# Slot logits of a fused attention and soft mixture of experts: small products from a transposed f16 copy of the attention output, in place of 32 extra columns of the value products

## The chip, the cores and the metric

The kernel runs on one core of a Trainium2 chip. The core has a matrix engine (PE, whose weight loads the profile lists apart as PEld), three engines for elementwise work and reductions (DVE, ACT, POOL) and a queue engine (SP) that issues most DMA transfers. Each engine works through its instructions in a fixed order and waits for others by semaphores. PE writes its results to PSUM, which DVE and ACT read; POOL works on SBUF only. The metric is the device time of one execution in microseconds (us); lower is better.

## The reference

Four batches of 12288 queries attend to 768 pooled keys, whose values are the keys themselves. The attention output x (49152 rows of 128) then goes through a soft mixture of experts with 32 slots. The slot logits `x @ phi` are what the change is about.

```python
kv_pool = kv.reshape(B, H // r, r, W // r, r, C).mean(axis=(2, 4))
k = v = kv_pool.reshape(B, -1, C) @ w_sr
s = scale * (q @ k.transpose(0, 2, 1))
a = np.exp(s - s.max(-1, keepdims=True))
x = (a / (a.sum(-1, keepdims=True) + 1e-09)) @ v
...
logits = x @ phi                                # 32 slots
d = softmax(logits over all rows)               # dispatch
slot_out = relu((d.T @ x) @ w1[e]) @ w2[e]      # per expert
out = softmax(logits over the slots) @ slot_out # combine
```

## The kernel before

The queries are cut into 96 blocks of 512 (`NB`), four blocks to a group; the last group is cut into one of three blocks and one of a single block, so that there are 25 groups. For each block:

- PE multiplies keys and queries into three PSUM tiles `s0`, `s1`, `s2` of two banks each (`qk`, L476 to L478: each operand is split into a high and a low part, so three products for each 128 keys, 18 of 512 columns in a block). There is one buffer of each, so the next block's products into `s0` wait until DVE has subtracted the maximum from this block's.
- DVE takes the row maximum: three reductions of 128x1024 (`rowmax1`, L483), a short reduction and a product (L493, L495), then a small PE product with a selector (`rowmax_pe`, L503), a reduction of its result (L508), and a transpose that spreads the maximum (`rowmax4`, L513). Four subtractions (`sub`, L521) then free the PSUM tiles. From L495 to L508 DVE waits for PE unless other DVE work is put there.
- ACT computes the exponential twice for each half of the block (`exp_hi` to f16, L528, and `exp_t` to f32, L532), POOL the low part of it as their difference (`plo`, L537).
- PE multiplies the probabilities with the values (`av_hi`, L554 and L555, and `av_lo`, L562): for each of four slices of 128 queries 12 products with the high part and 6 with the low part, 72 in a block. The right-hand side has 161 columns (160 in L555): one column of ones for the row sum, 128 of values, and 32 of `v @ phi`, which were made once per batch from a widened weight (`w_sb`, 160 columns: L368, and L799 at the start). The 32 last columns of the result are the slot logits before the division by the row sum.
- ACT copies the result, two slices at a time, from PSUM to the group's tile `xl` (`av_evac`, L572, 128x322).

The PSUM space outside `s0` to `s2` is two banks (`m0`, `m1`), which the value products, the row maximum's small product and all else share.

After the last block of a group, `group_ops` runs some twenty short steps: the logits are scaled into `LL` (`g1l`, POOL, L626), their column maximum is taken (L631, L633, L661 to L668, with a small PE product L654), weights are formed (L673 to L690) and 16 (for a full group) times two PE passes sum them with x (`g7m`, L707, 32 matmul records), which DVE adds to `acc` (L713). A reciprocal of the row sums (L609) is the DVE step near the start of it, and the row maximum for the combine (`k_max`, L718) a later one. Keys and values of the next batch are made while a batch runs (`kv_ops`; L347 to L440). After the last block come the experts and the combine.

The order on PE, DVE, ACT and POOL is made when the program is built: every step is an `op(...)` with a cost, a latency, a priority and its dependences and buffers; `Plan.emit` goes through them with these numbers and writes each engine's instructions in the order it finds. On the chip the order stands, and times are what they are. SP's queue is in order too: loads of q (1 MB for a group, two buffers) and of kv, then weights and results.

Of the kernel before, what the change touches and what calls it, by code (L numbers as in the profile page):

```python
# [172 lines left out]
def attention_then_soft_moe(ctx: ExitStack, tc: tile.TileContext, qT, kv0, kvT, w_sr, w_srT, phi, w1, w2, outT):  # L173
# [20 lines left out]
    FAST = len(GB) - 2  # L194
    VW = C + 1 + NS
# [40 lines left out]
    nc.vector.memset(epk, EPS * PK)  # L236
# [39 lines left out]
        "pooled": 1, "v32": 1, "r6": 2, "rq": 2, "m1": 2, "mb": 1, **{f"s{u}": 1 for u in range(NU)},  # L276
# [84 lines left out]
    def kv_v_mm(b, h):  # L361
        if h == 0:
            VU[b] = bp.tile([P, NT, C + NS], F32, tag="v32", name=f"v32_{b}", bufs=1)
        pv = mt([P, 512], f"pv_{b}_{h}")
        pv3 = PK_[b, h, "v"] = pv[:, : 3 * (C + NS)].rearrange("p (t c) -> p t c", t=3)
        for t in range(3):
            kt = 3 * h + t
            nc.tensor.matmul(pv3[:, t, :], pooled[b][:, kt * P : (kt + 1) * P], w_sb, start=True, stop=True)  # L368

    def kv_v_out(b, h):  # L370
        nc.scalar.activation(VU[b][:, 3 * h : 3 * h + 3, :], PK_.pop((b, h, "v")), AF.Copy, scale=1.0 / R2)

    def kv_m(b, k, h):
# [11 lines left out]
        if h and k:  # L385
            nc.vector.tensor_reduce(out=am2, in_=am, axis=X, op=ALU.max)
# [5 lines left out]
    def kv_s_mm(b):  # L392
        pa = PK_[b] = mt([P, 512], f"pa_{b}")
        nc.tensor.matmul(
            pa[:, : 2 * P], ones, AM.pop(b)[1].rearrange("p k n -> p (k n)"), start=True, stop=True
        )

    def kv_s_g(b):
        pa = PK_.pop(b)
        pg = pa[:, 2 * P : 2 * P + 2]  # L400
        nc.vector.tensor_reduce(out=pg, in_=pa[:, : 2 * P].rearrange("p (k n) -> p k n", k=2), axis=X, op=ALU.max)
# [138 lines left out]
    def av_tile(i, k):  # L540
        if k % 2 == 0 and i == NB - 1:
            PX[i, k // 2] = ps.tile([P, 2, BQ], F32, tag=f"s{k // 2}", name=f"px_{i}_{k}")[:, :, :VW]
        elif k % 2 == 0:
            px = mt([P, 512], f"px_{i}_{k}")
            PX[i, k // 2] = px[:, : 2 * VW].rearrange("p (n c) -> p n c", n=2)
        return PX[i, k // 2][:, k % 2, :]

    def av_hi(i, k):
        _, vhi, vlo = VU[i // BPB]
        px = av_tile(i, k)  # L550
        ks = slice(k * P, (k + 1) * P)
        for t in range(NT):
            p = PP[i, t // TH][0][:, t % TH, ks]
            nc.tensor.matmul(px, p, vhi[:, t, :], start=(t == 0), stop=False)  # L554
            nc.tensor.matmul(px[:, 1:], p, vlo[:, t, :], start=False, stop=False)  # L555

    def av_lo(i, k):
# [3 lines left out]
        for t in range(NT):  # L561
            nc.tensor.matmul(px, PP[i, t // TH][1][:, t % TH, ks], vhi[:, t, :], start=False, stop=(t == NT - 1))  # L562

    def av_evac(i, k):
# [3 lines left out]
        o = (i - GB[g][0]) * TB + 2 * k  # L568
        if i == NB - 2 and k == 0:
            nc.vector.tensor_copy(XL[g][:, o : o + 2, :], PX.pop((i, k)))  # L570
        else:
            nc.scalar.activation(XL[g][:, o : o + 2, :], PX.pop((i, k)), AF.Copy)  # L572
# [23 lines left out]
    def g0(g):  # L596
# [4 lines left out]
        if g > FAST:  # L601
            nc.vector.tensor_scalar_add(xc, xc, EPS * PK)
# [219 lines left out]
    def kv_ops(b, base, step, dep0, dep1):  # L822
# [10 lines left out]
        m = {0: [], 1: []}  # L833
        for h in range(2):
# [5 lines left out]
            for k in range(2):  # L840
                m[k].append(op("DVE", (0.53 if k == 0 else 0.2) + 0.2 * h * k, 0.08, p + step * (1 + 0.4 * k), [at_["vo", h]] + m[k] + m[0][:1], lambda h=h, k=k: kv_m(b, k, h), use=[("v32", b)]))
        d = [op("ACT", 0.4, 0.1, base + step * 5, m[0] + m[1], lambda k=k: kv_d(b, k)) for k in range(2)]
        s = op("PE", 0.6, 0.4, base + step * 5.5, d, lambda: kv_s_mm(b), acq=[("m", ("pa", b))])
        s = op("DVE", 1.1, 0.08, base + step * 5.5, [s], lambda: kv_s_g(b), use=[("m", ("pa", b))])
        prev = [s] + dep1
        for k in range(2):
# [3 lines left out]
            prev = [a]  # L850

    kv_ops(0, -60, 1.5, [[ops["pool", 0, R2 - 2], ops["wo"]], [ops["pool", 1, R2 - 2], ops["wo"]]], [])

    def group_ops(g):
# [5 lines left out]
        base = HEAD + (e + 2.6) * PER  # L860
# [5 lines left out]
        deps = [ops["x", e, 1]]  # L866
        if g >= 2:
# [21 lines left out]
        go("1l", big, bg(), [o["1u"]], g1l)  # L889
# [363 lines left out]
```

## Time and profile before

| | us |
|---|---|
| runs (two) | 1116.43 and 1115.16, median 1115.8 |
| profiled execution, first to last instruction | 1112.9 |
| PE busy / PEld busy | 1044.9 / 893.6 |
| DVE busy | 984.2 |
| ACT busy | 829.4 |
| POOL busy | 870.5 |

The profiled execution is one run of the program; its own time is known as the span alone, 2.9 us below the median of the runs. Busy shares are averages over a start that loads and pools the first keys (about 30 us), 96 blocks, and an end (from about 1005 us on) with the experts and the combine. Names of tiles are the program's, without buffer numbers; `m` is one of the two shared banks. A record of a matmul lasts longer than its place in the pipeline: what it costs is the distance from one start to the next.

### The profile page before, as it was taken

Reading aid. Unit: us, or ns where it says so; the run is one execution under the profiler, and the core shown is the slowest. Engines: PE = TensorE matmul, PEld = TensorE weight load, DVE = VectorE, ACT = ScalarE, POOL = GpSimd, SP = SyncE. Lnnn points to the kernel's source line nnn. Section 1 sums busy time; section 2 is a strip of 40 time slices with the busy share of each in tenths; the row PEclk is TensorE's granted clock in tenths of the full one; section 3 lists DMA queues with packets and bytes.
Section 4 is the critical chain, followed back from the end, with each engine's and each line's share of the span. In section 5 each row is a group of like instructions: output and inputs, shape, how many; then the busy total and the mean of one; then the engine's idle time right before and its main releaser. Section 6 shows DMA issues by size and latency. Waiting matters only on the chain.

```text
span 1112.9 us, 24732 instructions
## 1 busy us (share of the span) xinstructions
PE 1044.9 (94%) x10198; PEld 893.6 (80%) x10198; DVE 984.2 (88%) x1493; ACT 829.4 (75%) x1029; POOL 870.5 (78%) x503
## 2 busy tenths in 40 slices
PE   3699999999999999999999999999999999997885
PEld 2588888888888888888888888888888888886343
DVE  7889889899889989899888988989989988997894
ACT  1677778778777878778777788688778777875563
POOL 0679898798899889789899989789889889873440
PEclk9899999999999999999999999999999999999975
DMA  9218301111136310120145310120110110113498
GB/s 351 108 31 177 70 16 39 39 58 39 39 60 150 82 35 6 39 87 10 39 102 108 82 39 1 39 95 2 39 39 1 39 39 2 39 39 114 145 406 357
DMA packets 17407, 89.15 MB, mean 80 GB/s; under 512 B 1680, under 2 KB 3984, under 8 KB 11152
## 3 DMA queue, kind: packets, MB, share of 16 engines
q1 hardware_dynamic: 13408, 69.47, 17.0%
q0 software_dynamic: 3312, 17.70, 8.4%
q8 instruction: 81, 1.33, 0.5%
q10 hardware_dynamic: 576, 0.41, 0.1%
q14 instruction: 30, 0.25, 0.1%
HBM read 58.87 MB, written 25.17 MB: 76 GB/s over the span
## 4 chain that ended last, share of the span: by engine, by line
PE 61%; ACT 18%; DVE 15%; issue 3%; POOL 2%; DMA 1%; SPq 0%; DVEq 0%; ACTq 0%
PE m L562 10%; PE m L554 10%; PE m L555 9%; ACT phi L528 8%; PE s L476 8%; PE s L478 7%; PE s L477 7%; ACT t L532 7%; DVE t L521 4%; PE m L503 3%; DVE r L483 3%; PE m L707 2%; PE po L1138 2%; DVE o L1147 2%; DVE mb L513 1%
## 5 line engine op out<-in xcount | busy, mean ns | idle before, releaser
L537 POOL TENSOR_TENSOR plo<-t,phi 128x1536 f16<-128x1536 f32 x190 | 598.8, 3156 | 128.1 <-ACT t L532 127.3
L528 ACT ACTIVATE phi<-t,lnk 128x1536 f16<-128x1536 f32 x192 | 301.5, 1570 | 118.9 <-DVE t L521 118.7
L483 DVE TRANSPOSE_TENSOR_REDUCE r<-s 128x32 f32<-128x1024 f32 x288 | 348.6, 1233 | 29.3 <-PE s L478 25.7
L554 PE MATMUL m<-vhi,phi 128*128 128x161 f16 x2280 | 354.7, 234 | 2.8 <-DVE acc L713 1.4
L555 PE MATMUL m<-vlo,phi 128*128 128x160 f16 x2280 | 353.8, 233 | 0.0
L521 DVE TENSOR_TENSOR t<-s,mb 128x1024 f32<-128x1024 f32 (+1 forms) x384 | 342.8, 949 | 9.3
L532 ACT ACTIVATE t<-t,lnk 128x1536 f32<-128x1536 f32 x192 | 301.5, 1570 | 3.6
L476 PE MATMUL s<-qhi,khi 128*128 128x512 f32 x576 | 239.9, 417 | 6.1 <-DVE t L521 5.8
L554 PEld LDWEIGHTS <-phi 128*128 128x128 f16 x2304 | 224.3, 98 | 24.3 <-issue 24.3
L555 PEld LDWEIGHTS <-phi 128*128 128x128 f16 x2304 | 225.1, 98 | 5.4 <-issue 3.5
L562 PE MATMUL m<-vhi,plo 128*128 128x161 f16 x2280 | 226.5, 234 | 0.4 <-POOL plo L537 0.4
L478 PE MATMUL s<-qhi,klo 128*128 128x512 f32 x576 | 226.6, 393 | 0.0
L477 PE MATMUL s<-qlo,khi 128*128 128x512 f32 x576 | 226.1, 392 | 0.0
L562 PEld LDWEIGHTS <-plo 128*128 128x128 f16 x2304 | 178.2, 100 | 1.2 <-POOL plo L537 0.6
L466 POOL TENSOR_TENSOR qlo<-q,qhi 128x512 fp32r<-128x512 f32 x96 | 128.6, 1340 | 26.8 <-ACT qhi L462 26.8
L572 ACT ACTIVATE xl<-m 128x322 f32<-128x322 f32 x189 | 81.4, 430 | 84.5 <-PE m L562 83.8
L476 PEld LDWEIGHTS s<-qhi,khi 128*128 128x128 f32 x576 | 109.2, 190 | 32.6 <-issue 7.5
L478 PEld LDWEIGHTS s<-qhi,klo 128*128 128x128 f32 x576 | 108.8, 189 | 24.7 <-DVE klo L356 0.5
L477 PEld LDWEIGHTS s<-qlo,khi 128*128 128x128 f32 x576 | 109.5, 190 | 18.7 <-issue 0.7
L513 DVE STREAM_TRANSPOSE mb<-m 128x512 f32<-128x512 f32 x96 | 68.3, 711 | 3.3
L462 ACT ACTIVATE qhi<-q 128x512 fp32r<-128x512 f32 x96 | 59.1, 616 | 1.5 <-issue 0.8
L508 DVE TENSOR_REDUCE m<-m 128x16 f32<-128x64 f32 x96 | 21.5, 224 | 40.7 <-PE m L503 40.7
(145 smaller groups left out, 860.1 us busy)
## 6 DMA issues: line engine op xcount, KB each, us to landing
q<-qT SPq DMA_DIRECT2D x23, 1024.0 KB, 4.8
outT<-o SPq DMA_DIRECT2D x21, 1024.0 KB, 5.4
kva<-kvT POOLq DMA_DIRECT2D x9, 1536.0 KB, 11.2
kva<-kvT SPq DMA_DIRECT2D x3, 1536.0 KB, 10.5
kv<-kv SPq DMA_DIRECT2D x8, 512.0 KB, 5.6
w<-w SPq DMA_DIRECT2D x2, 1536.0 KB, 6.4
w<-w SPq DMA_DIRECT2D x4, 768.0 KB, 4.4
outT<-o SPq DMA_DIRECT2D x6, 512.0 KB, 4.7
```

Of the source, the lines that this page charges most:

```text
L466: nc.gpsimd.tensor_tensor(out=lo, in0=q_src(i), in1=hi.bitcast(F32), op=ALU.subtract)
L476: nc.tensor.matmul(s, khi[:, ks], hi, start=True, stop=False)
L477: nc.tensor.matmul(s, khi[:, ks], lo, start=False, stop=False)
L478: nc.tensor.matmul(s, klo[:, ks], hi, start=False, stop=True)
L483: nc.vector.tensor_reduce(out=MX[i][:, 2 * u : 2 * u + 2, :].rearrange("p t b -> p (t b)"), in_=S[i, u].rearrange("p t (b j) -> p (t b) j" ...
L521: nc.vector.tensor_tensor(out=TT_[i, h][:, o : o + n, :], in0=S[i, t // 2][:, u : u + n, :], in1=MX[i].unsqueeze(1).broadcast_to([P, n, BQ ...
L528: nc.scalar.activation(hi, TT_[i, h], AF.Exp, bias=lnk, scale=SCALE)
L532: nc.scalar.activation(t, t, AF.Exp, bias=lnk, scale=SCALE)
L537: eng.tensor_tensor(out=lo, in0=TT_.pop((i, h)), in1=PP[i, h], op=ALU.subtract)
L554: nc.tensor.matmul(px, p, vhi[:, t, :], start=(t == 0), stop=False)
L555: nc.tensor.matmul(px[:, 1:], p, vlo[:, t, :], start=False, stop=False)
L562: nc.tensor.matmul(px, PP[i, t // TH][1][:, t % TH, ks], vhi[:, t, :], start=False, stop=(t == NT - 1))
```

## The change

For blocks 0 to 91 (`i < OLD`) the value products have 129 and 128 columns. The logits of such a block come in five new steps: ACT scales the attention output by 1/2048 and rounds it to f16 (`x_hi`, twice a block, 128x256), DVE forms the f16 rest (`x_lo`, twice, 128x256, from PSUM), SP issues a DMA that transposes both parts (`x_t`, 128x1024 f16, 256 KB, SBUF to SBUF), PE multiplies four 128x128 pieces with the high and low parts of phi (`l_mm`, 12 products of 32 columns into a shared bank), and ACT copies the 128x128 result into `xl` (`l_out`). `av_evac` is two slices of 129 columns for these blocks. Blocks 92 to 95 keep the 32 extra columns; the last batch therefore keeps its 160-column weight, and the other three make 128 columns and one maximum instead of two.

Around it: `av_hi` is given to the order in pieces of two 128-key tiles (`AVS`), which it can place apart; phi is scaled and split once at the start (`phi_m` to `phi_l`); the group steps start later (3.1 instead of 2.6 block lengths) and `g1l` waits for all `l_out` of the group; and the descriptor memory of POOL's DMAs is set to 8192.

```diff
+    OLD = GB[FAST][0]
...
+        w = VWB(b) - 1
...
-            nc.tensor.matmul(pv3[:, t, :], pooled[b][:, kt * P : (kt + 1) * P], w_sb, start=True, stop=True)
+            nc.tensor.matmul(pv3[:, t, :], pooled[b][:, kt * P : (kt + 1) * P], w_sb[:, :w], start=True, stop=True)
...
+    def VWB(b):
+        return VW if b == B - 1 else C + 1
+
+    def NKS(b):
+        return 2 if b == B - 1 else 1
...
+    def wide(i):
+        return VW if i >= OLD else C + 1
...
-        for t in range(NT):
+        for t in range(t0, t0 + AVS):
             p = PP[i, t // TH][0][:, t % TH, ks]
-            nc.tensor.matmul(px, p, vhi[:, t, :], start=(t == 0), stop=False)
-            nc.tensor.matmul(px[:, 1:], p, vlo[:, t, :], start=False, stop=False)
+            w = wide(i)
+            nc.tensor.matmul(px, p, vhi[:, t, :w], start=(t == 0), stop=False)
+            nc.tensor.matmul(px[:, 1:], p, vlo[:, t, : w - 1], start=False, stop=False)
...
+    def x_hi(i, k):
+        if k == 0:
+            XF[i] = sp.tile([P, 2, TB, C], F16, tag="xs", name=f"xs_{i}")
+        nc.scalar.activation(XF[i][:, 0, 2 * k : 2 * k + 2, :], PX[i, k][:, :, 1:], AF.Copy, scale=XS)
+
+    def x_lo(i, k):
+        nc.vector.scalar_tensor_tensor(
+            out=XF[i][:, 1, 2 * k : 2 * k + 2, :], in0=PX[i, k][:, :, 1:], scalar=XS,
+            in1=XF[i][:, 0, 2 * k : 2 * k + 2, :], op0=ALU.mult, op1=ALU.subtract,
+        )
+
+    def x_t(i):
+        xs = XF.pop(i)
+        XF[i, "t"] = sp.tile([P, 2 * TB, P], F16, tag="xt", name=f"xt_{i}")
+        nc.sync.dma_start_transpose(out=XF[i, "t"], in_=xs.rearrange("p k t c -> p (k t c)"))
+
+    def l_mm(i):
+        xt = XF.pop((i, "t"))
+        pl = XF[i, "l"] = mt([P, 512], f"pl_{i}")
+        for k in range(TB):
+            out = pl[:, k * NS : (k + 1) * NS]
+            nc.tensor.matmul(out, xt[:, k, :], PHI["hi"], start=True, stop=False)
+            nc.tensor.matmul(out, xt[:, k, :], PHI["lo"], start=False, stop=False)
+            nc.tensor.matmul(out, xt[:, TB + k, :], PHI["hi"], start=False, stop=True)
+
+    def l_out(i):
+        src = XF.pop((i, "l"))[:, : TB * NS].rearrange("p (t s) -> p t s", t=TB)
+        nc.scalar.activation(x_of(i)[:, :, C + 1 :], src, AF.Copy)
...
-        base = HEAD + (e + 2.6) * PER
+        base = HEAD + (e + 3.1) * PER
...
+        lx = [ops["l", i] for i in range(s, s + n) if i < OLD]
...
-        go("1l", big, bg(), [o["1u"]], g1l)
+        go("1l", big, bg(), [o["1u"]] + lx, g1l)
...
+            if split:
+                h_ = op("ACT", act(2 * C), 0.1, p - 2, [a2], lambda: x_hi(i, u), acq=[xk] if u == 0 else [], use=[m] + ([xk] if u else []))
...
+            if split:
+                xls.append(op("DVE", dve(2 * C) + 0.1, 0.1, p - 2, [h_], lambda: x_lo(i, u), use=[m, xk]))
+        if k == TB - 1 and i < OLD:
+            q = p + XLAT
+            a = op("SP", 1.8, 3.0, q, xls[-2:] + [ops["phil"]], lambda: x_t(i), acq=[tk], use=[xk])
+            a = op("PE", 12 * 0.029, 0.17, q + 5, [a], lambda: l_mm(i), acq=[lk], use=[tk])
+            ops["l", i] = op("ACT", act(TB * NS), 0.1, q + 5, [a], lambda: l_out(i), use=[lk, x])
```

The new order is shown at three places. Names are tile, block and buffer number: `s_54_1` is the second score tile of block 54, `m1_115` and `m0_114` the shared banks, `xs` the f16 parts of x and `xt` their transpose.

On DVE, one block in the middle of the program, from the transpose that spreads the maximum to the product ahead of the next one, stood before as follows.

```order
L513 STREAM_TRANSPOSE mb_53_7676<-m1_53_7674 128x512
L521 TENSOR_TENSOR t_53_0_7691<-s_53_0_7572,mb_53_7676 128x1024
L521 TENSOR_TENSOR t_53_0_7691<-s_53_1_7603,mb_53_7676 128x512
L521 TENSOR_TENSOR t_53_1_7719<-s_53_1_7603,mb_53_7676 128x512
L521 TENSOR_TENSOR t_53_1_7719<-s_53_2_7616,mb_53_7676 128x1024
L483 TENSOR_REDUCE r6_54_7738<-s_54_0_7721 128x32
L483 TENSOR_REDUCE r6_54_7738<-s_54_1_7733 128x32
L609 RECIPROCAL r_12_7770<-xl_12_7253 128x16
L483 TENSOR_REDUCE r6_54_7738<-s_54_2_7745 128x32
L493 TENSOR_REDUCE m1_115<-r6_54_7738 128x16
L495 TENSOR_TENSOR rq_54_7795<-m1_115,quad_108 128x64
```

The same block on DVE after the change:

```order
L557 STREAM_TRANSPOSE mb_53_8686<-m1_53_8683 128x512
L636 SCALAR_TENSOR_TENSOR xs_51_8679<-m1_115,xs_51_8679 128x256
L565 TENSOR_TENSOR t_53_0_8706<-s_53_0_8573,mb_53_8686 128x1024
L565 TENSOR_TENSOR t_53_0_8706<-s_53_1_8594,mb_53_8686 128x512
L565 TENSOR_TENSOR t_53_1_8742<-s_53_1_8594,mb_53_8686 128x512
L565 TENSOR_TENSOR t_53_1_8742<-s_53_2_8605,mb_53_8686 128x1024
L527 TENSOR_REDUCE r6_54_8761<-s_54_0_8746 128x32
L636 SCALAR_TENSOR_TENSOR xs_51_8679<-m0_114,xs_51_8679 128x256
L527 TENSOR_REDUCE r6_54_8761<-s_54_1_8756 128x32
L527 TENSOR_REDUCE r6_54_8761<-s_54_2_8770 128x32
L537 TENSOR_REDUCE m0_114<-r6_54_8761 128x16
L539 TENSOR_TENSOR rq_54_8819<-m0_114,quad_108 128x64
```

Two `x_lo` of block 51 stand among the steps of blocks 53 and 54, one directly behind the transpose and one between two row-maximum reductions. Over the whole program 84 of the 184 stand first behind such a transpose, 7 between L539 and L552 (before: L495 and L508), and 93 elsewhere. Between L495 and L508 nothing stood in 71 of 96 blocks; between L539 and L552 nothing stands in 51, the reciprocal of the row sums in 14 and the long `k_max` reduction in 18 (before: 19).

On SP's queue, in the middle of the program, before:

```order
L451 DMA q_14_7157<-qT 128x2048
L451 DMA q_15_7731<-qT 128x2048
L451 DMA q_16_8308<-qT 128x2048
L451 DMA q_17_8865<-qT 128x2048
L451 DMA q_18_9429<-qT 128x2048
```

And after:

```order
L495 DMA q_14_8106<-qT 128x2048
L644 DMA_TRANSPOSE xt_47_8128<-xs_47_8032 128x8x128
L644 DMA_TRANSPOSE xt_48_8274<-xs_48_8180 128x8x128
L644 DMA_TRANSPOSE xt_49_8412<-xs_49_8383 128x8x128
L644 DMA_TRANSPOSE xt_50_8578<-xs_50_8536 128x8x128
L495 DMA q_15_8764<-qT 128x2048
```

Four transposing DMAs now stand between two loads of q, and the first of the four directly behind a load.

On PE, after the last key product of a block, the second half of a value slice and what follows it, before:

```order
L554 LDWEIGHTS phi_52_1_7614
L554 MATMUL m0_114<-vhi_2_6660,phi_52_1_7614 128x161
L555 LDWEIGHTS phi_52_1_7614
L555 MATMUL m0_114<-vlo_2_6661,phi_52_1_7614 128x160
L562 LDWEIGHTS plo_52_0_7620
L562 MATMUL m0_114<-vhi_2_6660,plo_52_0_7620 128x161
```

And after, at the end of the first value slice behind the key products of block 52:

```order
L610 LDWEIGHTS plo_50_1_8391
L610 MATMUL m1_115<-vhi_2_6746,plo_50_1_8391 128x129
L651 LDWEIGHTS xt_49_8412
L651 MATMUL m0_114<-phhi_158,xt_49_8412 128x32
L652 LDWEIGHTS xt_49_8412
L652 MATMUL m0_114<-phlo_174,xt_49_8412 128x32
L653 LDWEIGHTS xt_49_8412
L653 MATMUL m0_114<-phhi_158,xt_49_8412 128x32
```

The twelve small products (three of them shown) stand inside PE's stream of value products and wait there for the transposing DMA.

More of the change, by code (lines that the diff above doesn't have):

```diff
@@ L275, in attention_then_soft_moe @@
         "m": 2, "t": TBUF, "phi": PB, "plo": PB, "q": 2, "qs": 2, "xl": 2, "D": 1, "kv": 2,
-        "pooled": 1, "v32": 1, "r6": 2, "rq": 2, "m1": 2, "mb": 1, **{f"s{u}": 1 for u in range(NU)},
+        "pooled": 1, "v32": 1, "r6": 2, "rq": 2, "m1": 2, "mb": 1, "xs": 2, "xt": 2, **{f"s{u}": 1 for u in range(NU)},
     })
@@ L384, in kv_m @@
         )
-        if h and k:
-            nc.vector.tensor_reduce(out=am2, in_=am, axis=X, op=ALU.max)
+        if h and k == NKS(b) - 1:
+            nc.vector.tensor_reduce(out=am2[:, : k + 1], in_=am[:, : k + 1, :], axis=X, op=ALU.max)
     def kv_d(b, k):
@@ L393, in kv_s_mm, with two_power @@
         pa = PK_[b] = mt([P, 512], f"pa_{b}")
+        n = NKS(b)
         nc.tensor.matmul(
-            pa[:, : 2 * P], ones, AM.pop(b)[1].rearrange("p k n -> p (k n)"), start=True, stop=True
+            pa[:, : n * P], ones, AM.pop(b)[1][:, :n, :].rearrange("p k n -> p (k n)"), start=True, stop=True
         )
[L398 to L401, printed above, removed]
+    def two_power(pa, n, g, inv):
+        pg = pa[:, 2 * P : 2 * P + n]
+        nc.vector.tensor_reduce(out=pg, in_=pa[:, : n * P].rearrange("p (k n) -> p k n", k=n), axis=X, op=ALU.max)
@@ L408, in kv_s_g, with phi_m, phi_d, phi_mm @@
         VS[b] = (g, inv)
+    PHI = {}
+    def phi_m():
+        PHI["am"] = cp.tile([P, 1], F32, tag="pam", name="pam")
+        nc.vector.tensor_reduce(out=PHI["am"], in_=phi_sb, axis=X, op=ALU.max, apply_absolute_value=True)
+    def phi_d():
+        PHI["dg"] = bp.tile([P, 2, P], F32, tag="dg", name="dg_phi", bufs=1)[:, 0, :]
+        nc.scalar.activation(PHI["dg"], ident, AF.Copy, scale=PHI["am"])
+    def phi_mm():
+        PHI["pa"] = mt([P, 512], "pa_phi")
+        nc.tensor.matmul(PHI["pa"][:, :P], ones, PHI.pop("dg"), start=True, stop=True)
@@ L561, in av_lo @@
         for t in range(NT):
-            nc.tensor.matmul(px, PP[i, t // TH][1][:, t % TH, ks], vhi[:, t, :], start=False, stop=(t == NT - 1))
+            nc.tensor.matmul(px, PP[i, t // TH][1][:, t % TH, ks], vhi[:, t, : wide(i)], start=False, stop=(t == NT - 1))
     def av_evac(i, k):
@@ L850, in kv_ops @@
             prev = [a]
+        ops["tt", b] = ops["t", b, nk - 1]
+    a = op("DVE", 0.2, 0.08, -40, [], phi_m, at=10.0)
+    a = op("ACT", 0.4, 0.1, -40, [a], phi_d)
+    a = op("PE", 0.3, 0.4, -40, [a], phi_mm, acq=[("m", "phi")])
+    a = ops["phig"] = op("DVE", 1.1, 0.08, -40, [a], phi_g, use=[("m", "phi")])
+    a = op("ACT", 0.3, 0.1, -20, [a], phi_h)
+    ops["phil"] = op("DVE", 0.2, 0.08, -20, [a], phi_l)
     kv_ops(0, -60, 1.5, [[ops["pool", 0, R2 - 2], ops["wo"]], [ops["pool", 1, R2 - 2], ops["wo"]]], [])
@@ L983, in attention_then_soft_moe @@
             p = T0 + AVD * PER + 1.3 * k
-            a1 = op("PE", 12 * 0.0705, 0.17, p, prev + ([] if end else los), lambda i=i, k=k: av_hi(i, k), acq=[m] if k % 2 == 0 else [], use=pp + ([m] if k % 2 else []))
+            for t in range(0, NT, AVS):
+                a1 = op("PE", 2 * AVS * (0.0705 if i >= OLD else 0.0575), 0.17, p, prev + ([] if end or t else los), lambda i=i, k=k, t=t: av_hi(i, k, t), acq=[m] if k % 2 == t == 0 else [], use=pp + ([m] if k % 2 or t else []))
+                prev = [a1]
             ops["hv", k] = prev = [a1]
```

75 lines of the change are left out of this document (53 added, 22 removed).

## The prediction

> **What bounds the kernel now.** I read the busy shares by stretch first, then the waits, then DVE's timeline of one group of four blocks, and last the rows of single operations.
>
> Two stretches in the middle of the program; after the stretch stand its length and the busy time of PE, PEld, DVE, ACT and POOL, then PE's granted clock:
>
> ```profile
> 400.00:600.00 200.00, 197.17 (x1976) 173.28 (x1974) 180.90 (x271) 158.27 (x195) 171.31 (x97) 1.00 0.22 56
> 600.00:800.00 200.00, 197.94 (x1971) 173.69 (x1970) 180.28 (x266) 160.01 (x197) 173.58 (x99) 1.00 0.15 45
> ```
>
> PE looks like the bound at 99%, DVE second at 90%, and the clock is full. But a PE that waits inside a modelled matmul also looks busy, so I ask DVE what it waits for. Its two longest waits, over the whole program (us in total, times, longest), and the transposes that mark the blocks:
>
> ```profile
> DVE m L508 <- PE m L503: 40.7, 74, 0.6
> DVE r L483 <- PE s L478: 25.7, 34, 1.0
> L513 DVE STREAM_TRANSPOSE mb<-m x96: 711/711/714, 30.9 to 1004.6; 128x512 f32<-128x512 f32 x96
> ```
>
> The 96 transposes are (1004.6 - 30.9)/95 = 10.25 us apart. DVE's timeline of one group (start, us, what, idle time before it):
>
> ```profile
> 616.68 0.71 DVE L513 STREAM_TRANSPOSE mb<-m 128x512 f32<-128x512 f32 x1
> 617.50 3.55 DVE L521 TENSOR_TENSOR t<-s,mb 128x1024 f32<-128x1024 f32 x4
> 620.97 2.53 DVE L483 TRANSPOSE_TENSOR_REDUCE r<-s 128x32 f32<-128x1024 f32 x2
> 623.42 0.21 DVE L609 RECIPROCAL r<-xl 128x16 f32<-128x16 f32 x1
> 623.61 1.25 DVE L483 TRANSPOSE_TENSOR_REDUCE r<-s 128x32 f32<-128x1024 f32 x1
> 624.89 0.33 DVE L493 TENSOR_REDUCE m<-r 128x16 f32<-128x96 f32 x1
> 625.25 0.22 DVE L495 TENSOR_TENSOR rq<-m,quad 128x64 f32<-128x64 f32 x1
> 626.07 0.22 DVE L508 TENSOR_REDUCE m<-m 128x16 f32<-128x64 f32 x1 [0.59 <-PE m L503]
> 626.32 0.71 DVE L513 STREAM_TRANSPOSE mb<-m 128x512 f32<-128x512 f32 x1
> ...
> 636.21 0.23 DVE L508 TENSOR_REDUCE m<-m 128x16 f32<-128x64 f32 x1
> 636.47 0.71 DVE L513 STREAM_TRANSPOSE mb<-m 128x512 f32<-128x512 f32 x1
> ...
> 646.34 0.71 DVE L513 STREAM_TRANSPOSE mb<-m 128x512 f32<-128x512 f32 x1
> ...
> 651.75 1.25 DVE L483 TRANSPOSE_TENSOR_REDUCE r<-s 128x32 f32<-128x1024 f32 x1 [0.95 <-PE s L478]
> ...
> 657.15 0.71 DVE L513 STREAM_TRANSPOSE mb<-m 128x512 f32<-128x512 f32 x1
> ```
>
> The four blocks take 9.64, 10.15, 9.87 and 10.81 us. In the first, DVE goes from one step to the next without a gap but for the 0.59 us in which the selector product is made. That wait is a round trip, which a less busy PE hardly shortens. DVE's own chain thus sets three blocks in four; in the fourth PE is 0.95 us late with key products, the block in which the group's sums (L707) stand on PE. So the time is held by DVE, with PE close behind, and a change that takes from PE and gives to DVE has little to win: at most the 25.7 us.
>
> **The change, part by part.** PE's prices come from distances between starts:
>
> ```profile
> 515.37 0.23 PE L554 MATMUL m<-vhi,phi 128*128 128x161 f16 x1
> 515.44 0.23 PE L555 MATMUL m<-vlo,phi 128*128 128x160 f16 x1
> 515.51 0.19 PE L654 MATMUL m<-cb,sel_bf 128*128 128x4 bf16 x2
> 515.57 0.59 PE L562 MATMUL m<-vhi,plo 128*128 128x161 f16 x6
> ...
> 508.27 0.39 PE L476 MATMUL s<-qhi,khi 128*128 128x512 f32 x1
> 508.49 0.39 PE L477 MATMUL s<-qlo,khi 128*128 128x512 f32 x1
> ```
>
> A product of 161 columns costs 0.07 us, one of 512 columns 0.225, so about 0.44 ns a column. Two products of 4 columns with their weight loads take 0.06 us together, 0.03 each: that is the floor set by loading weights. Taking 32 columns away saves 32 x 0.44 = 14 ns, 72 times a block: 1.0 us. The bounds are 0 (if the weight loads set the pace at 128 columns) and this 1.0; I take 1.0, since the pair at 0.03 us is nearest to what a load alone costs. The twelve small products cost 12 x 0.03 = 0.36 us (at most 12 x 0.07 = 0.84). PE gains about 0.63 us a block, 58 us over 92 blocks, nearly all of it off the path.
>
> The Trainium skill, page "TensorE: Matmul & The Clock Gate", section "Back-to-back issue gap", speaks against the change: in a stream of weight loads and matmuls it gives about 81 ns for each product of 128 columns, set by both. By that figure PE's 72 products would take 72 x (81 - 70) = 0.8 us more instead of 1.0 less, and the program would follow PE to an estimated 1200 us. The trace has 161 columns at 70 ns already and so does not agree; the mechanism is kept as a rival below, priced from rows.
>
> DVE and ACT prices, from the whole trace with shapes apart (count, busy us, mean ns):
>
> ```profile
> L356 DVE SCALAR_TENSOR_TENSOR klo<-m,khi 128x256 fp32r<-128x256 f32 x4 | 1.5, 385 | 0.0
> L381 DVE TENSOR_REDUCE am<-v 128x1 f32<-128x96 f32 x8 | 1.9, 241 | 0.0
> L351 ACT ACTIVATE khi<-m 128x256 fp32r<-128x256 f32 x4 | 1.5, 378 | 3.4 <-PE m L347 3.4
> L572 ACT ACTIVATE xl<-m 128x322 f32<-128x322 f32 x189 | 81.4, 430 | 84.5 <-PE m L562 83.8
> L728 ACT ACTIVATE LL<-LL 128x128 f32<-128x128 f32 x1 | 0.3, 293 | 0.0
> ```
>
> `x_lo` is L356's operation in the same size, 385 ns from start to end, 184 times. What it adds depends on where it stands:
>
> - Between independent steps an operation overlaps its neighbours: the reciprocal of 0.21 us starts before the reduction ahead of it ends (620.97 + 2.53) and moves the next start by 0.19 us. So 0.31 to 0.385, I take 0.34: 93 x 0.34 = 31.6 us.
> - Behind the transpose a gap stands already: 617.50 - 616.68 = 0.82 us from start to start for an operation of 0.71, because the subtraction needs its result. An independent `x_lo` starts there about 0.08 us before the transpose ends, so that 0.11 to 0.17 us is added; I take 0.15: 84 x 0.15 = 12.6 us.
> - Between L495 and L508 seven stand in a wait of 0.59 us: 0.
>
> The sum is 44.2 us, with bounds 38 and 50. Off it come 14 reciprocals that now stand in that same wait (14 x 0.19 = 2.7 us), and six short maxima of three batches' second value part (6 x 0.24 = 1.4). The six short DVE steps for phi at the start lie in a time when DVE waits for the first keys: 0. And DVE's waits for key products should end: relative to DVE, PE gains 0.63 us and DVE itself gets about 0.45 us longer in a block, together more than the 0.95 us by which PE is late. I take all 25.7 us, with 10 as the other end. What is late next is then DVE alone.
>
> ACT gets 2 x 0.378 for `x_hi` and 0.29 for `l_out`, and saves 2 x 0.05 where 322 columns become 258: 0.95 us on a block of about 8.1 (158 to 160 in 200 us, 10.25 us a block). At 9.1 of 10.4 us it has 1.3 us left, which covers it; if that cover went, exponentials would come later and POOL's `plo`, 8.8 us a block, with them, and the five buffers of each stand between them and PE. POOL's steps don't change. `x_hi` and `x_lo` hold a shared bank about 0.9 us longer than one copy did; with 0.63 us less PE work the other bank covers that.
>
> The DMA has no row of its own. The nearest ones (KB each, us to landing):
>
> ```profile
> kv<-kv SPq DMA_DIRECT2D x8, 256.0 KB, 5.0
> kva<-kva POOLq DMA_DIRECT2D x3, 384.0 KB, 3.9
> q<-qT ACTq DMA_DIRECT2D x1, 256.0 KB, 7.6
> q<-qT SPq DMA_DIRECT2D x23, 1024.0 KB, 4.8
> ```
>
> SBUF to SBUF 384 KB took 3.9 us; 256 KB in a row behind others 5.0, at the crowded start 7.6. I take 5 us, by the row of equal size on the same queue; the ends are 3.9 and 7.6. In the order the closest demand is the transpose of block 49, issued about when block 52's key products start; the small products stand behind 18 key products (4.1 us) and 18 value products (1.0 us), 5.1 us later. At 5 us nothing waits. SP itself carries nothing else that is urgent: a load of q is needed a group later. One transpose in four stands right behind such a load: if the two share its rate, it lands after 4.8 x 1.25 = 6.0 us. In the order its products come 6 key products (1.4 us), 58 value products (58 x 0.056 = 3.2) and a selector product with its wait (0.3 to 0.8) later, so at 5 to 5.4 us, and PE is then up to 1 us late once a group, of which some 0.2 us are covered by DVE's subtraction; I leave this to the range (23 x 0.8 = 18 us at most).
>
> The Trainium skill, page "DMA: Bandwidth & Descriptors", section "Latency and other measured facts", puts transposing DMAs at 261 GB/s and the fixed cost near 2 us; by it the landing is an estimated 3 us, and the rival of a late transpose below would fall away. No run here shows it yet.
>
> **Sum.** 1112.9 + 44.2 - 2.7 - 1.4 - 25.7 = 1127 us of span. The runs' median lies 2.9 us above the profiled span: 1130. I add 1 us for the last group's later start: 1131 us, 1.4% slower. With the bounds of `x_lo` and of the ended waits this case reaches from 1124 to 1153, most likely 1124 to 1141.
>
> **Rivals.**
>
> - *The transpose lands late.* At 7.6 us PE waits 2.5 us in front of the small products. Behind these stand 18 more value products (1.0 us) and the selector product for which DVE waits anyway; some 0.4 us of slack there. DVE loses 2 us in one block of four: 23 x 2 = 46, so 1131 + 46 = 1177. It decides from a landing of about 5.5 us on; at 6.5 us the time is about 1154. For it: the closest demand is at 5.1 us. Against it: the 3.9 us row is the only one that stays in SBUF. Slower, 0.22.
> - *Products of 128 columns go no faster.* If the weight load sets the pace, PE keeps 0.07 us a product and gets 0.36 us: 197.5/200 x 10.25 + 0.36 = 10.5 us a block against 10.25, and its lateness stays: 1131 + 25.7 = 1157. Against it: the pair at 0.03 us. Slower, 0.06.
> - *`x_lo` is hidden.* If it fills gaps wherever it stands, at the lower ends 0.11 and 0.31 and with the remaining small gaps of DVE filled, 15 us less: about 1116, no change. 0.14.
> - *PE sets the time after all.* If DVE's chain stretched only because PE is slow throughout, the blocks would follow PE's 0.63 us: 1116 - 58 = 1058, or half of it, 1087, as DVE has to take in 0.45 us. Against it: the gapless 9.64 us block. Faster, 0.05.
>
> **How the numbers follow.** My case has 0.53, and falls on both sides of 2%, which is about what a measurement of this kernel can tell from no change (1138): 0.4 within, 0.13 slower. With the rivals: faster 0.05; within 0.4 + 0.14 = 0.54; slower 0.13 + 0.22 + 0.06 = 0.41. The range leaves out the faster case below 1114 and the worst of the late transpose above 1163.
>
> **What would show it.** Right: DVE busy about 1050 us and `x_lo` near 385 ns; PE's value products 0.056 us apart; waits of L483's successor for key products near 0; the wait of L508's successor at 30 to 35 us; four blocks at 41 to 41.5 us instead of 40.5. Wrong: value products still 0.07 us apart; PE or its weight loads waiting for the transposing DMA, with landings over 5.5 us; new DVE waits for ACT in front of `x_lo`; or blocks shorter than DVE's 9.64 us.

## Result and profile after

| | before | after |
|---|---|---|
| runs, median of two (us) | 1115.8 | 1232.65 (1230.95 and 1234.35) |
| ratio, 95% interval | | 1.104 [1.100, 1.109] |
| profiled execution, first to last instruction | 1112.9 | 1228.9 |
| PE / DVE busy | 1044.9 / 984.2 | 1036.6 / 1041.0 |
| ACT / POOL busy | 829.4 / 870.5 | 895.2 / 870.9 |

The change costs 10.4%; 1131 us with a range up to 1163 was predicted. The two stretches of the prediction again, after the change (length, busy time of PE, PEld, DVE, ACT, POOL, PE's granted clock, DMA share, GB/s):

```profile
400.00:600.00 200.00, 178.68 (x2051) 150.53 (x2050) 176.71 (x285) 158.65 (x229) 159.95 (x91) 0.97 0.27 59
600.00:800.00 200.00, 171.32 (x1912) 144.04 (x1911) 167.86 (x271) 152.47 (x224) 151.81 (x88) 0.96 0.40 87
```

No engine is full any more: PE fell from 99% to 89 and 86%, DVE from 90% to 88 and 84%, and the granted clock is below 1.00. When two engines both lose busy share, they wait for each other or for something third. DVE's waits over the whole program (us in total, times, longest), and the transposes that mark the blocks:

```profile
DVE xs L636 <- ACT xl L621: 48.6, 52, 18.1
DVE m L552 <- PE m L547: 40.9, 71, 0.9
DVE r L527 <- PE s L522: 23.9, 41, 3.6
DVE m L537 <- PE m L610: 13.9, 20, 1.0
...
L557 DVE STREAM_TRANSPOSE mb<-m x96: 711/711/712, 32.2 to 1116.0; 128x512 f32<-128x512 f32 x96
```

The second line is the selector's round trip, unchanged. The first and the fourth are new, the third (key products) should have gone and stayed. Of the first, 35 us are four waits of 3.8 to 18.1 us that follow late transposes; without the transposes (e1 below) the line is 13.2 us. PE's two longest waits are for the transposing DMA and for the subtraction that frees `s0`:

```profile
PE m L651 <- DMA xt<-xs: 41.5, 11, 17.3
PE s L520 <- DVE t L565: 38.7, 45, 2.9
```

Before, the second of them was:

```profile
PE s L476 <- DVE t L521: 5.8, 2, 3.4
```

From the first transpose to the last it takes 1083.8 us where it took 973.7: 110 of the 117 us lie inside the blocks. Two kinds of place stand out.

**A stall.** PE's timeline at 366 us, and the DMA view of the stretch 359 to 384 us (GB/s in 40 slices, then what was issued, count, KB each, us to landing):

```profile
365.96 0.22 PE L603 MATMUL m<-vlo,phi 128*128 128x128 f16 x1
383.48 0.21 PE L651 MATMUL m<-phhi,xt 128*128 128x32 f16 x1 [17.30 <-DMA xt<-xs]
```

```profile
GB/s 10 0 170 118 328 419 367 320 190 73 164 144 153 156 229 144 153 256 154 173 186 145 160 25 74 32 29 46 21 20 41 20 20 20 41 17 13 11 5 0
...
kva<-kvT POOLq DMA_DIRECT2D x2, 1536.0 KB, 17.0
q<-qT SPq DMA_DIRECT2D x1, 1024.0 KB, 8.4
xt<-xs SPq DMA_TRANSPOSE x1, 22.5
```

A load of q, a load of kv that POOL's queue accumulates, and a transpose were issued within 1.3 us of each other. The transpose landed after 22.5 us; in the last third of that time the DMA engines moved some 20 GB/s. PE stood for 17.3 us. Over the whole program the 92 transposes landed as follows, and in the stretch from 820 to 1000 us, where no kv is loaded, the longest took 4.3 us:

```profile
DMA to landing us min/median/max: 3.0/3.1/22.5
```

Ten took over 6 us. All ten were in flight together with a transfer that POOL's queue accumulates (a load of kv, or a fold of kv in SBUF), and eight of them landed within 1 us after that transfer did.

**A steady group.** Groups 18 to 22, beside which no kv is loaded, take 44.3 to 44.6 us (before 40.4 to 40.5), in four blocks of about 10.7, 10.2, 10.5 and 13.0. The last block of one of them begins so on DVE:

```profile
894.09 0.71 DVE L557 STREAM_TRANSPOSE mb<-m 128x512 f32<-128x512 f32 x1
894.79 0.42 DVE L636 SCALAR_TENSOR_TENSOR xs<-m,xs 128x256 f16<-128x256 f32 x1
895.54 0.43 DVE L636 SCALAR_TENSOR_TENSOR xs<-m,xs 128x256 f16<-128x256 f32 x1 [0.33 <-ACT xl L621]
895.88 3.54 DVE L565 TENSOR_TENSOR t<-s,mb 128x1024 f32<-128x1024 f32 x4
900.18 1.25 DVE L527 TRANSPOSE_TENSOR_REDUCE r<-s 128x32 f32<-128x1024 f32 x1 [0.75 <-PE s L522]
```

and on PE, with the granted clock of the stretches around it (column 8 of a row, ahead of DMA share and GB/s):

```profile
897.24 0.77 PE L520 MATMUL s<-qhi,khi 128*128 128x512 f32 x1 [1.53 <-DVE t L565]
897.81 0.63 PE L521 MATMUL s<-qlo,khi 128*128 128x512 f32 x1
898.23 0.63 PE L522 MATMUL s<-qhi,klo 128*128 128x512 f32 x1
...
901.19 0.39 PE L521 MATMUL s<-qlo,khi 128*128 128x512 f32 x1
901.41 0.39 PE L522 MATMUL s<-qhi,klo 128*128 128x512 f32 x1
```

```profile
895.70:897.20 1.50, 0.02 (x1) 0.00 (x0) 1.50 (x3) 0.28 (x1) 1.50 (x1) 1.00 0.02 7
897.20:900.60 3.40, 3.36 (x8) 2.71 (x9) 2.65 (x4) 2.78 (x2) 0.36 (x2) 0.50 0.41 79
900.60:903.00 2.40, 2.40 (x13) 1.75 (x12) 1.99 (x2) 1.85 (x2) 1.94 (x1) 0.99 0.04 7
```

Two `x_lo` stand between the transpose and the subtraction that frees `s0`. The subtraction starts 1.79 us after the transpose, not 0.82; 0.33 us of that is the second `x_lo`'s wait for ACT. PE has done its value products by then and waits 1.53 us, and after this wait it runs at half its clock for 3.4 us: key products are 0.43 us apart and not 0.225. DVE then waits 0.75 us for them.

The prices of single operations came out close to the estimates, on PE by the distance between starts, and for `x_lo` in the view of groups (count, busy us, mean ns, idle time before it and what ended it):

```profile
906.67 0.22 PE L602 MATMUL m<-vhi,phi 128*128 128x129 f16 x1
906.73 0.22 PE L603 MATMUL m<-vlo,phi 128*128 128x128 f16 x1
906.79 0.22 PE L602 MATMUL m<-vhi,phi 128*128 128x129 f16 x1
...
917.85 0.18 PE L651 MATMUL m<-phhi,xt 128*128 128x32 f16 x1 [0.32 <-DVE m L552]
917.88 0.18 PE L652 MATMUL m<-phlo,xt 128*128 128x32 f16 x1
```

```profile
L636 DVE SCALAR_TENSOR_TENSOR xs<-m,xs 128x256 f16<-128x256 f32 x184 | 75.6, 411 | 49.0 <-ACT xl L621 48.6 <-PE m L372 0.2
```

Value products are 0.056 us apart, small products 0.025, and `x_lo` takes 411 ns (385 expected).

### The profile page after: what moved, and what is told of

Same layout as the page of the kernel before. It is cut to its first block, busy times and chain, and to the rows that moved or that the text cites. A ratio compares the mean times of both kernels' runs of the same rounds, so it can differ in the third digit from the quotient of the medians.

```text
span 1228.9 us, 27819 instructions
## 1 busy us (share of the span) xinstructions
PE 1036.6 (84%) x11304; PEld 853.6 (69%) x11304; DVE 1041.0 (85%) x1681; ACT 895.2 (73%) x1299; POOL 870.9 (71%) x501
## 4 chain that ended last, share of the span: by engine, by line
PE 48%; DVE 23%; ACT 18%; DMA 8%; issue 3%; POOL 0%; DVEq 0%; SPq 0%; ACTq 0%
DMA xt<-xs 8%; PE s L520 8%; PE m L602 7%; DVE t L565 7%; PE m L610 7%; PE s L521 6%; PE s L522 6%; PE m L603 6%; ACT phi L572 6%; ACT t L576 5%; DVE r L527 5%; DVE xs L636 2%; ACT xs L633 2%; PE m L547 2%; ACT xl L621 2%
## 5 line engine op out<-in xcount | busy, mean ns | idle before, releaser
L602 PE MATMUL m<-vhi,phi 128*128 128x129 f16 (+1 forms) x2280 | 309.7, 222 | 19.3 <-ACT xl L657 11.6
L603 PE MATMUL m<-vlo,phi 128*128 128x128 f16 (+1 forms) x2280 | 308.5, 221 | 0.0
L520 PE MATMUL s<-qhi,khi 128*128 128x512 f32 x576 | 249.7, 434 | 39.4 <-DVE t L565 38.7
L521 PE MATMUL s<-qlo,khi 128*128 128x512 f32 x576 | 233.9, 406 | 0.0
L610 PE MATMUL m<-vhi,plo 128*128 128x129 f16 (+1 forms) x2280 | 195.1, 222 | 0.0
L610 PEld LDWEIGHTS <-plo 128*128 128x128 f16 x2304 | 149.9, 99 | 0.7 <-issue 0.7
L633 ACT ACTIVATE xs<-m 128x256 f16<-128x256 f32 x184 | 69.8, 379 | 76.1 <-PE m L610 42.7
L636 DVE SCALAR_TENSOR_TENSOR xs<-m,xs 128x256 f16<-128x256 f32 x184 | 75.6, 411 | 49.0 <-ACT xl L621 48.6
L651 PE MATMUL m<-phhi,xt 128*128 128x32 f16 x368 | 37.3, 177 | 54.0 <-DMA xt<-xs 41.5
L621 ACT ACTIVATE xl<-m 128x258 f32<-128x258 f32 (+1 forms) x189 | 72.2, 382 | 6.5 <-DVE m L552 5.1
```

Of the source, the lines that this page charges most:

```text
L520: nc.tensor.matmul(s, khi[:, ks], hi, start=True, stop=False)
L521: nc.tensor.matmul(s, khi[:, ks], lo, start=False, stop=False)
L602: nc.tensor.matmul(px, p, vhi[:, t, :w], start=(t == 0), stop=False)
L603: nc.tensor.matmul(px[:, 1:], p, vlo[:, t, : w - 1], start=False, stop=False)
```

## Experiments

Times without an interval are single executions; the kernel before beside them took 1116.7 to 1117.4 us. Ten executions of one kernel (e17, below) lay between 1117.8 and 1122.1, so differences of 4 us and less mean nothing. Theory A: transposes in flight beside POOL's accumulating transfers land late and stop PE. Theory B: `x_lo` ahead of the subtractions lets PE run dry, and its clock falls. Rival C: neither; `x_lo`'s own time and the longer hold on the shared banks. "Steady group" is the median over groups 18 to 22 of the time from one transpose to the one four blocks on.

**No transfers (e1).**

```diff
-        nc.sync.dma_start_transpose(out=XF[i, "t"], in_=xs.rearrange("p k t c -> p (k t c)"))
+        XF[i, "t"] = XF.pop(i).rearrange("p k t c -> p (k t) c")
```

> Leaves out the 92 transposing DMAs: the small products read the untransposed parts of x as their weights, so the slot logits are not those of the reference; every other engine keeps its instructions and their order. Theory A (transposes that share the DMA engines with the accumulating loads of kv land late and stop PE): the six groups of four blocks with such a wait (47.7, 46.4, 61.5, 48.5, 51.8 and 48.8 us) fall to the 42.6 to 44.4 of the others, 44 us in all, about 1187 us. If late transposes were the whole miss, the time would come down to the predicted 1131. Theory B (x_lo ahead of the subtractions lets PE run dry for 1.5 us and the clock then falls): the steady groups stay at 42.6 to 44.5 us, granted clock in the middle 0.97 to 0.98 and not 1.00.

`xs` gets four buffers in place of two here and in the other runs without transfers, because the small products read it directly. 1184.3 us; steady group 44.4. Theory A's number: the transfers cost 48 us, and steady groups don't feel them.

**No accumulating loads of kv (e2).**

```diff
-            nc.gpsimd.dma_start(
-                out=kvs[b], in_=kvT[b - 1, :, c * KVC : (c + 1) * KVC, :], accum_op=ALU.add,
...
+            pass
```

> Leaves out the nine loads of kv that POOL's queue accumulates onto the first one (the pooled keys of batches 1 to 3 are wrong); the transposing DMAs stay. Theory A: transposes then land in 3.0 to 6 us everywhere, those behind a load of q the longest, PE waits for them under 5 us in all, and the time is about 1187 us, as without the transposes. Rival (the transposes are late by themselves, behind loads of q or on SP's queue): landings over 8 us remain and the time stays above 1215.

1200.4 us, between the kernel with all transfers and the one without, and between the two numbers expected. The longest landing fell from 22.5 to 10.9 us and PE's wait from 41.5 to 14.6 us (6 times). The four landings over 6.5 us that are left (8.1 to 10.9) stand beside the folds of kv in SBUF, which POOL's queue also accumulates and which this kernel keeps. With a load of q alone beside it a transpose took at most 6.4 us here (7.3 in e3).

**Small products later (e3).**

```diff
-            a = op("SP", 1.8, 3.0, q, xls[-2:] + [ops["phil"]], lambda: x_t(i), acq=[tk], use=[xk])
+            a = op("SP", 1.8, 12.0, q, xls[-2:] + [ops["phil"]], lambda: x_t(i), acq=[tk], use=[xk])
```

> The order is planned with 12 us for the transposing DMA and not 3, so the small products stand later on PE. Theory A: landings beside the accumulating loads remain at 6 to 22 us, but PE's waits for them fall from 43 us to 10 to 15 (the longest landing is still over 12), so about 1195 to 1200 us. If the late landing cost nothing, 1229.

1181.8 us, better than expected. PE waits 13.2 us for transfers, nearly all in one place (a landing of 24.6 us). But the steady group fell too, to 41.9 us: the new order has `x_lo` twice ahead of the first subtraction in 2 blocks, not in 14. So the experiment changed two things, and its 51 us can't be given to the landing alone.

**Subtraction first (e4).** The plan gives every step that holds a shared bank 60 points of urgency (`URGE`); `x_lo` loses them.

```diff
-                xls.append(op("DVE", dve(2 * C) + 0.1, 0.1, p - 2, [h_], lambda: x_lo(i, u), use=[m, xk]))
+                xls.append(op("DVE", dve(2 * C) + 0.1, 0.1, p - 2 + URGE, [h_], lambda: x_lo(i, u), use=[m, xk]))
```

> x_lo loses its urgency in the plan, so that on DVE most subtractions stand ahead of the second x_lo of a block. Theory B: PE's waits of 1.5 us for the subtraction go, the steady groups fall from 44.4 to about 42.5 us and the clock in undisturbed stretches returns to 1.00: 10 to 16 groups by 2 us, 1195 to 1210 us, with the late transposes still in it. Rival C (x_lo's own time and the shared banks held longer set the steady groups, not the order): longer held banks give back what PE gains, 1225 to 1235 us.

1206.7 us; steady group 41.1, and the granted clock from 870 to 1070 us is 1.00 again. A block on DVE now reads:

```profile
915.75 0.71 DVE L557 STREAM_TRANSPOSE mb<-m 128x512 f32<-128x512 f32 x1
916.39 0.38 DVE L636 SCALAR_TENSOR_TENSOR xs<-m,xs 128x256 f16<-128x256 f32 x1
916.70 3.53 DVE L565 TENSOR_TENSOR t<-s,mb 128x1024 f32<-128x1024 f32 x4
920.15 0.40 DVE L636 SCALAR_TENSOR_TENSOR xs<-m,xs 128x256 f16<-128x256 f32 x1
```

One `x_lo` behind the transpose moves the subtraction from 0.82 to 0.95 us after it, which is harmless. The second stands behind all four subtractions.

**Both plan changes (e5).**

> Both plan changes at once: 12 us planned for the transposing DMA, and x_lo without urgency. If late transposes (theory A) and x_lo ahead of the subtractions (theory B) are the two separate causes, their gains add up to nearly all of the miss: steady groups at 41 to 42 us, waits for the transposing DMA at 5 to 15 us, 1135 to 1150 us. If the two are one cause seen twice, it stays near the better of the two alone, 1175 to 1185 us.

1189.9 us: a miss. PE no longer waits for transfers, but steady groups take 44.1 us, with a first block of up to 14.7. In this order DVE has a new wait:

```profile
DVE m L537 <- ACT xs L633: 16.8, 11, 2.3
```

L537 writes into a shared bank, and in those blocks it stands behind value products that `x_hi` has not yet read. The order is made anew with every edit of a cost, and two gains need not add up.

**No transfers, subtraction first (e6).**

> Leaves out the transposing DMAs (the slot logits are wrong) and takes x_lo's urgency away. By theories A and B nothing of the miss is left: 1126 to 1135 us, as predicted at first, groups at 41 to 42 us, clock 1.00 in the middle. Rival C (longer held banks and ACT's two more steps cost by themselves): 1150 us or more, with waits for the shared banks in every group.

1149.8 us, 34.5 us less than with urgent `x_lo`: theory B's share. The 14 blocks with two `x_lo` ahead of the subtraction take 172.5 us together in e1 and 146.5 here, so 26 of the 34.5 us lie in them. The clock in the undisturbed stretch, urgent and not:

```profile
820.00:1000.00 180.00, 161.56 (x1815) 136.88 (x1813) 158.71 (x249) 141.93 (x202) 141.30 (x80) 0.96 0.08 25
```

```profile
820.00:1000.00 180.00, 167.73 (x1968) 144.33 (x1965) 170.42 (x269) 152.45 (x224) 151.99 (x84) 1.00 0.07 25
```

It is not the 1126 to 1135 expected but the 1150 of rival C. So some 15 to 24 us of the miss lie in a third place.

**Narrow products alone (e7)**, in the order of the kernel before:

```diff
-            nc.tensor.matmul(px, p, vhi[:, t, :], start=(t == 0), stop=False)
-            nc.tensor.matmul(px[:, 1:], p, vlo[:, t, :], start=False, stop=False)
+            w = VW if t == 0 or i >= 92 else C + 1
+            nc.tensor.matmul(px[:, :w], p, vhi[:, t, :w], start=(t == 0), stop=False)
+            w = VW if i >= 92 else C + 1
+            nc.tensor.matmul(px[:, 1:w], p, vlo[:, t, : w - 1], start=False, stop=False)
...
```

The products of `av_lo` are cut in the same way.

> The kernel before with its order unchanged, but in blocks 0 to 91 68 of the 72 value products have 129 or 128 columns (only the first product of a slice still adds to the logit columns, so the slot logits lack most of their parts). The prediction's step: PE leaves the path, DVE's 25.7 us of waits for key products end and nothing else moves, 1090 us (1085 to 1100), groups near 39.5 us. If PE sets the time after all: 1058 to 1087. If products of 128 columns go no faster: 1116.

1103.4 us: 13 us gained, half of what the prediction counted on. PE is busy for 57 us less, but DVE's waits for key products only fall from 25.7 us to:

```profile
DVE r L483 <- PE s L478: 17.8, 28, 1.3
```

**No `x_lo` (e9)**, in the kernel of e6 (no transfers, `x_lo` not urgent): the body of `x_lo` is left out and the order kept.

> The kernel without transposing DMAs and without x_lo's urgency (1149.8 us), and x_lo left out as well, with all other instructions in the same order; the small products read the high part of x in its place (the slot logits are wrong). It measures the term of the sum that x_lo was given, 44 us with bounds of 38 and 50. If the term was right: 1106 us (1100 to 1112). If x_lo costs what the undisturbed groups suggest (0.9 to 1 us more for eight of them than in e7, 0.12 us each): 22 us, about 1128.

1136.4 us, above both numbers expected. `x_lo` costs 13.4 us, where the sum had 44. What DVE doesn't do it waits: in front of the second step of the row maximum, for a shared bank (count, busy us, mean ns, idle before it and what ended it),

```profile
L537 DVE TENSOR_REDUCE m<-r 128x16 f32<-128x96 f32 x96 | 31.6, 329 | 30.6 <-PE m L610 19.9 <-ACT xs L633 6.9 <-DVE r L527 0.5
```

a wait that the kernel before did not have. Between 1103 (narrow products) and this, 33 us are left, although DVE has the same work in both.

**No `x_lo`, whole slices (e14)**, `AVS = 6` in place of 2.

> e9 (no transfer, no x_lo, 1136.4 us) with the value products of a slice given to the plan as one piece, as before the change, not in three. If the finer pieces make DVE wait for the shared banks: L537's 27 us of waits fall below 10 and the time to about 1118. If the small products' need of a bank does: within 4 us of 1136.

1136.7 us, as expected if the finer pieces of the value products have no part in it.

**No `x_lo`, no small products (e15).** `l_mm` is left out, `l_out` copies a constant.

> e9 with the twelve small products of a block left out; l_out copies a constant from SBUF, so that ACT's work and the order of all else stay and only PE's 0.3 us and the hold on a shared bank go. If that hold is the cause: DVE's waits in front of L537 (27 us) nearly vanish and the time falls to 1108 to 1115. If they stay, the order of the value products is the cause, and the time stays within 5 us of 1136 (PE's 0.3 us a block lie beside DVE's work).

1114.2 us, 22 us less, but by neither reason given: the wait in front of L537 hardly changed,

```profile
L537 DVE TENSOR_REDUCE m<-r 128x16 f32<-128x96 f32 x96 | 31.6, 329 | 29.2 <-PE m L610 18.1 <-ACT xs L633 6.8 <-ACT LL L803 0.5
```

and the time fell all the same. PE's busy time fell from 1003.4 to 980.0 us, by 23 us, about as much as the program's. So the small products do cost time. Whether it is PE's own 0.25 us a block or the shared bank that they hold until ACT has copied their result is not shown. A wait of PE for that copy went with them; in e9 it was:

```profile
PE m L602 <- ACT xl L652: 12.7, 27, 0.6
```

**`x_lo` on POOL (e8).** The engine computes it from the f32 copy of x, one step a block; 12 us are planned for the transposing DMA, as in e3.

```diff
+    def x_lo(i):
+        nc.gpsimd.tensor_tensor(
+            out=XF[i][:, 1], in0=x_of(i)[:, :, 1 : C + 1], in1=XF[i][:, 0], op=ALU.subtract
+        )
```

> x_lo is formed on POOL from the f32 copy of x (one step of 128x512 a block, 12 us planned for the transposing DMA), so DVE gets no new work. DVE's theory: groups back at 40 to 40.5 us and 1110 to 1120 us with 5 to 15 us of late transposes in it. Rival: POOL becomes the bound; 92 steps of about 1.1 us bring it from 870 to 970 us of busy time, about 10.1 us a block, and with its own waits 1130 to 1150 us.

1128.5 us, above the 1110 to 1120 expected, and 53 us below e3, where `x_lo` is on DVE (the order differs too); steady group 40.0, below the 40.45 before. POOL takes it (967.4 us busy, 1.17 us a step) without becoming the bound. The end behind the last transpose is 8.6 us longer than before, 116.9 us. So blocks 88 to 91 got the wide products back (e10):

> x_lo on POOL as in e8 (1128.5 us), and blocks 88 to 91 also keep the 32 extra columns, so that the last full group does not wait for small products. In e8 the end behind the last block took 116.9 us where the kernel before took 108.3; if that came from the last group's late logits, it falls to about 109 us and the time to 1120 to 1122. Rival: the end is late because the group steps start later, 1126 to 1129.

1123.8 us, a little over the range expected, the end 107.3: the late logits were what made it long. Then the start of the group steps as before the change (e12):

> As e10, and the group steps start 2.6 block lengths behind the group as in the kernel before, not 3.1. If the later start is what makes the end long, 1117 to 1120 us; if it was the logits of blocks 88 to 91, as e10.

1119.2 us, as expected, but not for the reason given: the end stayed at 107.8 us, and the 4.5 us, hardly more than the spread of single executions, came inside the blocks. Two variations of it, 8 us planned for the transfer (e13) and whole slices (e16):

> As e12, with 8 us planned for the transposing DMA and not 12. Undisturbed landings of 3 to 6 us still fit; beside accumulating loads PE waits more: 2 to 8 us more than e12, unless the order gains from the smaller distance.

> e12 (x_lo on POOL, 1119.2 us) with the value products of a slice as one piece. If the finer pieces cost time wherever they stand, about 1110; if not, within 4 us of 1119.

1125.2 us, in the expected range, and 1126.3 us, a miss: whole slices cost 7 us here, where in e14 they changed nothing. The same kernel as e12 was timed in more executions, with two earlier starts of the group steps beside it:

> The kernel of e12 (x_lo on POOL, blocks 88 to 91 with the 32 extra columns, 12 us planned for the transposing DMA, group steps at 2.6 block lengths), timed. Its steady groups take 40.0 to 40.8 us and those before 40.45, so no difference: ratio 1.000 to 1.004. If PE's relief were free of what takes it back (13 us in e7), 0.99.

> As e17, group steps at 2.4 block lengths. The order of the small products changes with it; within 6 us of e17 either way, and below the kernel before only if the small products come to stand where DVE doesn't wait for PE.

> As e17, group steps at 2.2 block lengths; the small products stand as in e17. The last group ends earlier: 0 to 4 us less than e17.

1119.05 us, ratio 1.0026 [1.0015, 1.0037]: no difference that matters, and not faster. The earlier starts gave 1.0099 [1.0078, 1.0119] at 2.4 block lengths and 1.0061 [1.0041, 1.0081] at 2.2; both missed what was expected. No whole version of the change ran below the kernel before.

## Why the prediction was wrong

The kernels form a chain, each with one more part of the change (us):

| step | time | adds |
|---|---|---|
| kernel before | 1116.7 | |
| narrow value products | 1103.4 | -13 |
| `x_hi`, `l_out`, new order, later group steps | 1114.2 | +11 |
| twelve small products a block | 1136.4 | +22 |
| `x_lo` on DVE, not urgent | 1149.8 | +13 |
| `x_lo` urgent, ahead of the subtractions | 1184.3 | +35 |
| transposing DMAs | 1232.7 | +48 |

The shares hold in this order of adding; taken from the other end they differ (taking the urgency away with the transfers still there gives 26 us, not 35).

- **"I take 5 us" for the landing, with ends of 3.9 and 7.6.** The centre was too high and the end far too low: the step counted on 5 us and no wait, and PE waited for a transfer 11 times, 41.5 us in all. Undisturbed, a transfer landed after 3.1 us. The estimate of 3 us from the Trainium skill, page "DMA: Bandwidth & Descriptors", section "Latency and other measured facts", agrees with this. The step failed because I priced neighbours only on SP's queue, and wrote "SP itself carries nothing else that is urgent". POOL's accumulating transfers, which have rows in the same view, were in flight beside all ten late transposes. The rival of the late transpose had nearly the right price (46 us against 48) by luck, as its mechanism was another: not 2 us in one block of four, but ten landings of 6.5 to 22.5 us.
- **"Behind the transpose a gap stands already ... I take 0.15."** For DVE this is right (0.13 in the block above). The step failed because only DVE's time was counted: what is behind `x_lo` on that engine is the subtraction that frees `s0`, and PE waits for it. The order shown ahead of the prediction had one `x_lo` there; 14 blocks have two (the second ones were priced among the 93 elsewhere), and one block of each steady group is of this kind. The urgency, with the order that came of it, costs 35 us. The lower clock after PE's wait is part of that: in e1 8 of the 14 blocks have a stretch at half clock and take 12.9 to 13.1 us, and the 6 without one take 10.9 to 11.7, so about 1.5 us each time and 12 us in all.
- **"DVE's own chain thus sets three blocks in four ... PE gains about 0.63 us a block ... nearly all of it off the path."** This is the reading on which the sum stood, and it fell on both sides. Taking PE's work away gave 13 us and not 25.7; adding the small products (0.25 us of PE's work a block, and a hold on a shared bank) cost 22 us and not 0; taking `x_lo` from DVE gave 13 us and not 44. The engines form a loop: PE needs `s0` from DVE, DVE needs the key products, then a shared bank that PE's value products must leave, then the selector product. A gapless DVE timeline showed that DVE was not waiting at that moment; it didn't show that PE's order could be changed without making it wait.
- **"I take all 25.7 us."** Narrow products ended 8 us of it. What stays fits PE's timeline before: the group's sums (L707, 1.09 us) stand between key products there, after `s0` was freed, where shorter value products don't help. In e7 the wait behind these sums is still there once a group, 0.6 us where it was 0.95, and makes up most of the 17.8 us. No run moved the sums.
- **"With 0.63 us less PE work the other bank covers that."** The longer hold on a shared bank was put at nothing. DVE's waits for a bank in front of L537 are new: 13.9 us behind value products alone in the changed kernel, some 27 us in e9. What they cost in time was not measured apart.
- **"I add 1 us for the last group's later start."** The end behind the last transpose grew by 4.5 us in the changed kernel (5.5 in e15, half of its step of 11 us), by 8.6 in e8; wide products for blocks 88 to 91 brought it back.
- **Right:** 14 ns saved on a value product, the small products' 0.03 us, `x_lo`'s duration (411 ns against 385), and that products of 128 columns do go faster. ACT's cover is open: its 66 us more of work have no term of their own in the table, but `x_lo` waits for ACT 13.2 us even without the transfers, one of the signs of being wrong that the prediction named.
- **The range** ended at 1163 because each rival was priced as a case that comes alone. Three costs came together, one of them (the subtraction) was on no list, and `x_lo`'s 44 us, too high by 31, hid part of the miss.

## What to carry to other kernels

When an instruction is put in front of another on one engine, ask first what the second one frees, and which engine idles until it does; the instruction's own time is the smaller part of its price. A transfer's landing is to be priced against everything that the DMA engines carry at that time, from all queues, and its consumer placed with that landing in mind. Where two engines hand buffers back and forth in a short loop, neither is "off the path" because the other looks full: take the work away from each in turn and measure.

## What the runs showed of the hardware

- A transposing DMA of 256 KB landed after 3.1 us alone, 6.5 to 9.1 us beside one accumulating load of 1536 KB on POOL's queue, 13.0 and 22.5 us when a load of q was in flight as well; in the last case the accumulating load itself took 22.6 us (10.8 to 13.5 in the eight others). It was seen again in e3: 24.6 us, the accumulating load 24.5, the load of q 12.0. Why the rate falls to 20 GB/s in the last third was not found.
- After a wait of PE of 1.53 us, with 0.46 us of another one shortly before, the granted clock was 0.50 for 3.4 us. Of nine waits of 1.53 us in the changed kernel seven were followed by half-speed key products. The trace shows what parts them: all 42 stretches of the granted clock in this program start on one grid of 3.413 us. In the seven cases one step of this grid held 1.51 to 1.98 us in which PE stood idle; in the two that escaped the idle time was split over two steps, with at most 1.53 us in one. Among the blocks of the changed kernel (from 60 us on), 13 steps at full clock were followed by half clock, with 1.51 us of idle time or more, and 275 were not, all but two of them with less than 1.5 and none with more than 1.72. The Trainium skill, page "TensorE: Matmul & The Clock Gate", section "Part 1: The HAM clock gate", gives the slow state after an idle window of about 3.4 us that runs freely; the free grid and its length agree with it, but here about half a window of idle time was enough.
- POOL formed 128x512 differences from f32 and f16 in SBUF in 1.17 us beside its other work, and its share rose to 86% without a loss to the other engines that the steady groups show.
